# Operands at multiples of 128 bytes, and 64-byte gaps between the homes of the split weights

## The chip, the cores and the metric

The kernel runs on one core of a Trainium2 chip. The metric is the device time of one execution in microseconds. Five engines work side by side: PE (TensorE, matmuls; its weight loads are listed as PEld), DVE (VectorE), ACT (ScalarE), POOL (GpSimd) and SP (SyncE, which issues the DMAs). They meet in SBUF, a memory of 128 partitions in which an operand is a range of bytes in every partition, and in PSUM, where PE puts its sums. This change moves operands within SBUF, so the start of an operand is given here in bytes from the start of the partition.

## The reference

One transformer block on x of 1 x 2048 x 448 in float32: layer norm, attention with 16 query heads of 28 and a single key and value head, residual; layer norm, a gated feed-forward with 1792 hidden columns, residual.

```python
x = A_x
h = x + _A_ref(_layernorm(x), A_wq, A_wk, A_wv, A_wo)
h2 = h + _B_ref(_layernorm(h), B_w1, B_w3, B_w2)
# _A_ref: p = softmax(q k^T * Dh**-0.5); (p v) @ wo
# _B_ref: gate = x @ w1; up = x @ w3; (silu(gate) * up) @ w2
```

## The kernel before

**Tiling.** The 2048 rows are four row tiles of 512 (`T`); the 448 columns are three chunks of 128 and one of 64. To keep nearly float32 accuracy with PE's faster rounded type, most products are made from a split of each operand into a rounded high part and the rest: high x high, low x high and high x low. `mm_D` (line 156) issues these for one output of 128 x 512 as eleven matmuls: three with the high input `xh` and the high weights, three with the low input `xl` and the high weights, three with `xh` and the low weights, and two for the 64-column chunk, in which `xh` holds both parts. PE streams the moving operand (here the input) past the stationary one (here 128 columns of weights); each matmul has its own weight load, which runs while the matmul before it streams.

**Stages.** Projections of q, k and v at the start (line 163 with the output `pb`); attention, where for each of 256 steps the scores of four heads are made from `KS` and the queries `qs` (line 367, each matmul on 32 partitions), ACT takes their exponentials into the tiles `pt`, `xh` and `xl` (line 374) and PE multiplies these with `VA` (line 383); beside that, ahead of time, the row maxima (line 283, then DVE at lines 293 and 311); the output projection (`wo_rows`, also line 163, moving `WO`, stationary `OS`, 448 columns); and from about 752 us on the feed-forward alone.

**The feed-forward.** For each row tile and each of 14 blocks of 128 hidden columns: `split_w` (DVE and POOL) splits the block's 128 columns of w1 and w3 into two homes, one for the high and one for the low part; `ffn1` makes gate (w1) and then up (w3) with 22 matmuls of 512 columns at line 163, moving `xh` and `xl`, the transposed normalised input; ACT and DVE make silu(gate) x up and split it into the tile `pt`; `ffn2` multiplies it with the split w2 (tile `w2s`) in 12 matmuls of 448 columns at line 990, for the block before. All this is written in a fixed order by hand, with splits two blocks ahead.

**Where operands lie.** The pool `keep` lays tiles one behind the other in the order of their first use, each padded to 32 bytes. `qs_tile` (line 84) hands out homes in turn. A home has 4096 bytes per partition; within it the four chunks of a weight block stand 1024 bytes apart, and in each chunk 512 bytes of w1 and then 512 of w3 (`put_w13`, line 88: index `m` 0 and 1). In the feed-forward the order of homes is

```python
homes, n_qs = [5, 6, 1, 2, 3, 4, 0], [0]     # line 945
```

Block 0 takes homes 5 and 6, block 1 homes 1 and 2; then one home goes to a split of w2, and from block 2 on each block takes the next two: 4 and 0, 5 and 6, 1 and 2, 3 and 4, 0 and 5, 6 and 1, 2 and 3, and again from 4 and 0. So home 5 serves blocks 0, 3, 6, 10, 13, 17, 20 and so on, in steps of 3 and 4. The input tiles (`xh`, `xl`, pool `xt`) follow behind the homes; their chunks are 2048 bytes apart.

Before the change `pexp` and `warm_t` hold 16 bytes each. Behind `pexp` everything stands 32 bytes past a multiple of 128; behind `warm_t`, which comes after home 5, it stands 64 past one. In memory the homes lie in the order 5, 6, 0, 1, 4, 2, 3, then the input. Home numbers, and starts by the layout of the built program:

| operand | start before | mod 128 | start after | mod 128 |
|---|---|---|---|---|
| KS, first of two | 45984 | 32 | 46080 | 0 |
| w2s (also KS, second) | 54176 | 32 | 54272 | 0 |
| OS, WO, QR, VA | | 32 | | 0 |
| home 5 | 141984 | 32 | 142080 | 0 |
| home 6 | 146112 | 64 | 146240 | 64 |
| home 0 | 150208 | 64 | 150400 | 0 |
| home 1 | 154304 | 64 | 154560 | 64 |
| home 4 | 158400 | 64 | 158720 | 0 |
| home 2 | 162496 | 64 | 162816 | 0 |
| home 3 | 166592 | 64 | 166976 | 64 |
| xh, first of two | 170688 | 64 | 171136 | 0 |
| pt holding the hidden block | 212416 or 220608 | 64 | 212864 or 221120 | 0 or 64 |

The distance from the input to the weights, modulo 1024, is the same for all chunks, since the chunks of either lie multiples of 1024 apart. Before, it is 0 for w1 and 512 for w3 in six homes, and 992 and 480 in home 5.

Of the kernel before, what the change touches and what calls it, by code (L numbers as in the profile page):

```python
# [8 lines left out]
F32 = mybir.dt.float32  # L9
F32R = mybir.dt.float32r  # L10
AF = mybir.ActivationFunctionType
# [5 lines left out]
P = 128  # L17
# [5 lines left out]
T = 512  # L23
NT = S // T
NQ = T // P
# [10 lines left out]
def block_kernel(  # L36
# [13 lines left out]
    ve, se, ge, pe, sy = nc.vector, nc.scalar, nc.gpsimd, nc.tensor, nc.sync  # L50
# [4 lines left out]
    def f(ap):  # L55
        return ap.bitcast(F32)


    keep = ctx.enter_context(tc.tile_pool(name="keep", bufs=1))
# [7 lines left out]
    X = [keep.tile([P, NQ, D], F32, name=f"X{t}") for t in range(NT)]  # L67
    ident = keep.tile([P, P], F32, name="ident")
    NEG = [keep.tile([P, 32], F32R, name=f"neg{k}") for k in range(2)]
    pexp = keep.tile([P, NQ], F32, name="pexp")  # L70
    KS = [keep.tile([P, S], F32R, name=f"KS{k}", tag=f"ks{k}") for k in range(2)]
    VA = keep.tile([P, NC, 32], F32, name="VA")
    QR = [keep.tile([P, NG, T], F32, name=f"QR{t}") for t in range(NT)]
# [9 lines left out]

    def qs_tile():
        k, n_qs[0] = homes[n_qs[0] % len(homes)], n_qs[0] + 1
        return keep.tile([P, 2, T], F32R, name="qs", tag=f"q{k}")

    def put_w13(k, tl):
        fl = tl.rearrange("p a b -> p (a b)")
# [53 lines left out]
    def bank(name="pb"):  # L143
        k = min(free, key=lambda k: order[k])
        free.remove(k)
        ps = ps_w.tile([P, T], F32, name=name, tag=f"bank{k}")
        used[id(ps)] = ps, k
        ready.pop(id(ps), None)
        return ps

    def done(ps, at=None):
        k = used.pop(id(ps))[1]
        order[k] = ready.get(id(ps), clock.end) + 0.7 if at is None else at
        free.append(k)

    def mm_D(ps0, ps, lhs, rhs, lsl, rsl, between=None, pairs_ab=((0, 0), (1, 0), (0, 1))):

        terms, rsl_n = [], rsl.stop - rsl.start
        for a, b in pairs_ab:
            terms += [(a, c, b, c) for c in range(3)]  # L160
        terms += [(0, 3, 0, 3), (0, 3, 1, 3)]
        for k, (a, ca, b, cb) in enumerate(terms):
            pe.matmul(  # L163
                ps, lhs[b][:, cb, lsl], rhs[a][:, ca, rsl],
                start=(k == 0), stop=(k == len(terms) - 1),
            )
            clock.mm("full", 0, ps0, 0.0182 + rsl_n / 2400, k == 0)
            if between is not None and k == 5:
                between()

    def load_w(dst, w):
        sy.dma_start(dst[:, 0:3], w[0:384].rearrange("(c p) m -> p c m", p=P))
        sy.dma_start(dst[0:64, 3], w[384:448])
        sy.dma_start(dst[64:128, 3], w[384:448])

    def load_w13(k):
        for m, w in enumerate((w1, w3)):
            load_w(W13[k][:, :, m], w[:, k * P : (k + 1) * P])

    def load_w2(k):  # L180
# [32 lines left out]
    XT = {}  # L213
# [43 lines left out]
    def build_qs(i, ps=None):  # L257
        t, g = divmod(i, NG)
        q = QS[i] = qs_tile()
        if ps is None:  # L260
            if i < 3:
                se.activation(q[:, 0], QR[t][:, g], AF.Copy)
            else:
                ge.tensor_copy(q[:, 0], QR[t][:, g])
            ge.tensor_tensor(q[:, 1], QR[t][:, g], f(q[:, 0]), op=ALU.subtract)
        else:
            se.activation(q[:, 0], ps, AF.Copy)
            ve.tensor_tensor(q[:, 1], ps, f(q[:, 0]), op=ALU.subtract)
# [170 lines left out]
    def split_w(k):  # L439
        wh, wl = [qs_tile().rearrange("p a (c m e) -> p (a c) m e", c=2, m=2)  # L440
                  for b in range(2)]
        ve.tensor_copy(wh, W13[k])
        ge.tensor_tensor(wl, W13[k], f(wh), op=ALU.subtract)
        return wh, wl
# [3 lines left out]
    def split_w2(k):  # L448
        if k == 0 and not w2s_home:
            w2s = qs_tile()  # L450
        else:
            if not w2s_home:
                w2s_home.append(keep.tile([P, 2, 2, T], F32R, name="w2s", tag="ks1"))
            w2s = w2s_home[0][:, k % 2]
        ve.tensor_copy(w2s[:, 0, :D], W2[k])
        ge.tensor_tensor(w2s[:, 1, :D], W2[k], f(w2s[:, 0, :D]), op=ALU.subtract)  # L456
        return w2s

    PAIRS = (0, 1)
    KD = keep.tile([P, 2, T], F32R, name="KD", tag="q5")  # L460
    warm_t = keep.tile([P, NQ], F32, name="warm_t")
    KDS = {0: KD[:, 0]}
    ab_t = keep.tile([P, 2, T], F32, name="ab", tag="q6")
    ab_pool, n_ab = [ab_t[:, k] for k in range(2)], [0]
    for h in range(2):
        sy.dma_start(X[0][:, 2 * h : 2 * h + 2], xv[0][:, 2 * h : 2 * h + 2])
    make_identity(nc, ident)
    ge.memset(pexp, -0.5)
    se.activation(warm_t, pexp, AF.Copy)

    with tc.tile_pool(name="start", bufs=1) as sp:
        wq_r = wo_r = OT[:, :, :D]
# [301 lines left out]
    p_pool = ctx.enter_context(tc.tile_pool(name="pt", bufs=1))  # L774
# [1 line left out]
    more, n_pt, n_ring = xt_tiles(), [0, 0], [0]  # L776

    def pt_new(k):
        return p_pool.tile([P, 2, T], F32R, name="pt", tag=f"pt{k}")

    def pt_ring():
        k, n_ring[0] = n_ring[0] % 4, n_ring[0] + 1
        return pt_new(k)

    def pt_tile(p):
        k, n_pt[p] = n_pt[p] % 3, n_pt[p] + 1
        return pt_new(2 * k + p) if k < 2 else more[p][:, :2]
# [36 lines left out]
    for t in range(NT - 1):  # L824
        for k in range(2):
            at(NC * NG * (t + 1) + 13 + k, load_w13, 2 * t + k)
# [144 lines left out]
    def ffn1(t, k, W):  # L971
        ps = [bank("pa"), bank("pa")]
        for m in range(2):
            mm_D(ps[m], ps[m], [w[:, :, m] for w in W], XT[t], slice(0, P), slice(0, T))
        sg = f(pt_ring()[:, 0])
        se.activation(sg, ps[0], AF.Silu)  # L976
        done(ps[0])
        ve.tensor_tensor(sg, ps[1], sg, op=ALU.mult)  # L978
        done(ps[1])
        h = pt_ring()  # L980
        se.activation(h[:, 0], sg, AF.Copy)  # L981
        ve.tensor_tensor(h[:, 1], sg, f(h[:, 0]), op=ALU.subtract)
        HID[t, k] = h[:, 0], h[:, 1]
# [17 lines left out]
    tl = NT - 1  # L1001
# [7 lines left out]
    for k in range(2):  # L1009
        on(0, 2.5, load_w13, 2 * tl + k)  # L1010
# [4 lines left out]
    for k in range(8, NF):  # L1015
        on(0, 2 if k < 10 else 4.5, load_w13, k)
        on(0, 4.5, load_w2, k)
# [8 lines left out]
    for t in range(NT):  # L1026
        for k in range(NF):
            end = t == tl and k >= NF - 2
            t2, k2 = divmod(NF * t + k + 2, NF)
            if t2 < NT:  # L1030
                WH[t2, k2] = split_w(k2)
            ffn1(t, k, WH.pop((t, k)))
            for fn, args in after.get((t, k), []):
                fn(*args)
            if prev is not None and not end:
                for n in range(NQ):
                    ffn2(*prev, n)
                if prev[1] == NF - 1:
                    for n in range(NQ):
                        y_out(prev[0], n)  # L1040
            t2, k2 = divmod(NF * t + k + 1, NF)
            if t2 < NT and not end:
                WS[t2, k2] = split_w2(k2)
            for fn, args in after.get((t, k + 0.5), []):
                fn(*args)
            prev = (t, k)
# [36 lines left out]
```

## Time and profile before

| | us |
|---|---|
| median of 3 runs | 1182.97 |
| lowest and highest | 1182.55 and 1183.31 |
| the profiled execution | 1182.28 |
| its span, first to last instruction | 1180.5 |

| stage, us from the span's start | PE busy | DVE | ACT | POOL |
|---|---|---|---|---|
| 0 to 100, start and first row maxima | 95.30 | 81.75 | 59.91 | 35.50 |
| 100 to 700, attention | 598.70 | 533.51 | 567.84 | 72.29 |
| 700 to 740, its last steps | 39.56 | 3.19 | 39.44 | 9.01 |
| 740 to 752 | 12.00 | 4.49 | 3.69 | 4.69 |
| 752 to 1180, feed-forward | 424.64 | 160.99 | 74.28 | 204.00 |

How to read it: a line of the profile names a source line (L163), an engine, an operation, the tiles written and read (`pa<-xh,qs`: moving xh, stationary qs, into PSUM tile pa) and a count. Matmuls follow one another while the one before still drains, so what a matmul costs is the distance from its start to the next start, not its own length. The chain of waits, listed in order of time, gives these distances summed over a stretch of equal matmuls.

### The profile page before, as it was taken

The page shows a single profiled execution, that of the slowest core. Times are in us where ns is not written, and L with a number is a line of the kernel's source. Part 1 is how long each engine was busy: PE and PEld are TensorE (multiplying, and loading weights), DVE is VectorE, ACT ScalarE, POOL GpSimd, SP SyncE. Part 2 cuts the span into 40 slices and gives each one's busy share as a digit, 9 for nine tenths or more (in the row PEclk, how much of TensorE's full clock was granted, in tenths as well). Part 3 has the DMA queues.
Part 4 walks back from the last instruction along what each step waited for, and adds up shares of the span by engine and source line. Part 5 has one row for each costly group of instructions (what it writes and reads, how often), then busy time and mean ns, then how long its engine had stood idle before and what let it go on. Part 6 is the DMA issues. An engine that isn't in the chain of part 4 may idle for free.

```text
span 1180.5 us, 22184 instructions
## 1 busy us (share of the span) xinstructions
PE 1170.2 (99%) x8618; PEld 746.3 (63%) x8618; DVE 783.9 (66%) x1479; ACT 745.2 (63%) x1435; POOL 325.5 (28%) x240
## 2 busy tenths in 40 slices
PE   8999999999999999999999999999999999999998
PEld 6664444446444445444455443788888888888887
DVE  8878999997999988989987961544343333433332
ACT  5649999996999997999998999312111111211111
POOL 5312001111110111110013013344555545455552
PEclk9999999999999999999999999999999999999999
DMA  4010100011000011000011000242000000000000
GB/s 165 10 37 2 42 12 9 19 24 37 19 19 10 12 23 38 19 19 17 5 42 35 2 18 19 79 114 59 1 32 1 1 24 9 1 1 32 1 1 31
DMA packets 35050, 30.58 MB, mean 26 GB/s; under 512 B 11905, under 2 KB 29569, under 8 KB 34945
## 3 DMA queue, kind: packets, MB, share of 16 engines
q1 hardware_dynamic: 34944, 29.17, 8.6%
q8 instruction: 67, 1.10, 0.4%
q14 instruction: 39, 0.31, 0.1%
HBM read 20.37 MB, written 3.80 MB: 20 GB/s over the span
## 4 chain that ended last, share of the span: by engine, by line
PE 95%; ACT 2%; DVE 2%; issue 1%; DMA 0%; POOLq 0%; POOL 0%; ACTq 0%
PE pa L163 27%; PE po L383 21%; PE pb L367 19%; PE pb L990 11%; PE pa L283 11%; PE pb L163 4%; PE pb L238 1%; ACT OT L390 1%; ACT ab L304 1%; ACT pt L374 0%; DVE mx L293 0%; DMA X<-in_A_x_dram 0%; DVE X L994 0%; ACT xh L374 0%; DVE st L192 0%
## 5 line engine op out<-in xcount | busy, mean ns | idle before, releaser
L293 DVE TENSOR_REDUCE mx<-pa 128x1 f32<-128x512 f32 x689 | 440.3, 685 | 22.6 <-PE pb L367 13.1
L367 PE MATMUL pb<-qs,KS 32*128 32x512 f32 x3072 | 385.4, 425 | 0.0
L374 ACT ACTIVATE pt<-pb 128x512 f32<-128x512 f32 x684 | 366.3, 622 | 12.5 <-PE pb L367 9.2
L367 PEld LDWEIGHTS pb<-qs,KS 32*128 32x128 f32 x3072 | 234.1, 182 | 132.6 <-ACT pt L374 68.1
L283 PE MATMUL pa<-KS,qs 32*128 32x512 f32 x886 | 312.1, 459 | 1.3
L163 PE MATMUL pa<-xh,qs 128*128 128x512 f32 x896 | 232.7, 392 | 0.0
L283 PEld LDWEIGHTS pa<-KS,qs 32*128 32x128 f32 x886 | 139.0, 182 | 83.7 <-DVE mx L293 46.5
L163 PEld LDWEIGHTS pa<-xh,qs 128*128 128x128 f32 x896 | 168.1, 188 | 35.4 <-issue 0.8
L383 PE MATMUL po<-pt,VA 128*32 128x512 f32 x1368 | 182.2, 604 | 0.4 <-ACT pt L374 0.4
L978 DVE TENSOR_TENSOR pt<-pa,pt 128x512 f32<-128x512 f32 x56 | 38.7, 691 | 209.3 <-PE pa L163 204.6
L976 ACT ACTIVATE pt<-pa 128x512 f32<-128x512 f32 x56 | 33.5, 597 | 195.1 <-PE pa L163 195.0
L990 PE MATMUL pb<-w2s,pt 128*128 128x448 f32 x660 | 145.0, 368 | 0.2 <-POOL w2s L456 0.2
L414 POOL TENSOR_TENSOR OT<-OT,rb 128x512 f32<-128x512 f32 x15 | 19.2, 1281 | 456.0 <-DMA rb<-sd 229.0
L981 ACT ACTIVATE pt<-pt 128x512 fp32r<-128x512 f32 x56 | 35.4, 633 | 153.6 <-DVE pt L978 149.3
L990 PEld LDWEIGHTS pb<-w2s,pt 128*128 128x128 f32 x660 | 122.8, 188 | 13.4 <-POOL w2s L456 0.6
L311 DVE CUSTOM_DVE_ANT_0 ab<-pa,ab 128x512 f32<-128x512 f32 x138 | 93.7, 687 | 39.7 <-PE pa L283 31.8
L374 ACT ACTIVATE xh<-pb 128x512 f32<-128x512 f32 x170 | 104.7, 634 | 0.0
L374 ACT ACTIVATE xl<-pb 128x512 f32<-128x512 f32 x170 | 99.8, 611 | 7.6 <-PE pa L283 5.3
L163 PE MATMUL pa<-xl,qs 128*128 128x512 f32 x336 | 95.1, 391 | 0.0
L383 PE MATMUL po<-xl,VA 128*32 128x512 f32 x340 | 89.4, 605 | 0.0
L383 PE MATMUL po<-xh,VA 128*32 128x512 f32 x340 | 89.4, 605 | 0.0
L304 ACT ACTIVATE ab<-pa 128x512 f32<-128x512 f32 x138 | 82.3, 608 | 6.7 <-PE pa L283 5.0
(109 smaller groups left out, 1084.0 us busy)
## 6 DMA issues: line engine op xcount, KB each, us to landing
rb<-sd SPq DMA_DIRECT2D x64, 64.0 KB
QR<-OT SPq DMA_DIRECT2D x60, 56.0 KB
QR<-in_B_w_dram SPq DMA_DIRECT2D x16, 192.0 KB
X<-in_A_x_dram SPq DMA_DIRECT2D x3, 896.0 KB
out_dram<-X SPq DMA_DIRECT2D x3, 896.0 KB
w<-in_B_w_dram SPq DMA_DIRECT2D x8, 192.0 KB
w_wo<-in_B_w_dram SPq DMA_DIRECT2D x6, 224.0 KB
qs<-mr SPq DMA_DIRECT2D x64, 2.0 KB
```

Source lines behind the costliest of these rows:

```text
L163: pe.matmul(ps, lhs[b][:, cb, lsl], rhs[a][:, ca, rsl], start=(k == 0), stop=(k == len(terms) - 1),)
L283: pe.matmul(ps, QS[i][r, 0, n * P : (n + 1) * P], KS[0][r, kt * T : (kt + 1) * T] if keys is None else keys[r], start=True, stop=True)
L293: ve.tensor_reduce(self.to(), ps, axis=AX.X, op=ALU.max)
L304: se.activation(self.ab, ps, AF.Relu)
L311: ve.tensor_tensor_reduce(self.ab, ps, self.ab, 1.0, -3.0e38, ALU.add, ALU.max, self.to())
L367: pe.matmul(self.ps, KS[k % 2][r, c * P : (c + 1) * P], QS[i][r, k // 2], start=(k == 0), stop=(k == 2))
L374: se.activation(f(PT[i, c, p][:, jj]), self.ps, AF.Exp, bias=0.0, scale=SCALE)
L383: pe.matmul(PO[i][32 * j : 32 * j + 32], VA[:, c], f(PT[i, c, j // 2][:, j % 2]), start=(c == 0), stop=(c == NC - 1))
L976: se.activation(sg, ps[0], AF.Silu)
L978: ve.tensor_tensor(sg, ps[1], sg, op=ALU.mult)
L981: se.activation(h[:, 0], sg, AF.Copy)
L990: pe.matmul(Y[t][n][:, :D], hid[a][:, n * P : (n + 1) * P], w2s[:, b, :D], start=(k == 0 and m == 0), stop=(k == NF - 1 and m == 2))
```

## The change

It does four things. `pexp` grows to 128 bytes and takes the place of `warm_t`, so that what follows it starts at a multiple of 128. A new function `shift` allocates a tile of 64 bytes the first time a home is handed out, for all homes but number 4 and for the first of the `pt` tiles used, so that the next tile starts 64 bytes further. `load_w13` writes w3 into the first half of each chunk and w1 into the second, and `ffn1` reads them with `1 - m`, so that gate is still made first. Nothing else is added or removed: the sequence of instructions on PE, DVE and POOL is the same, ACT's first ACTIVATE writes another tile, and SP issues the loads of w3 ahead of those of w1.

After it, the distance from the input to the weights modulo 1024 is, for w1 and w3: home 5 128 and 640, home 6 192 and 704, home 0 256 and 768, home 1 320 and 832, homes 4 and 2 384 and 896, home 3 448 and 960.

```diff
-    pexp = keep.tile([P, NQ], F32, name="pexp")
+    pexp = keep.tile([P, 32], F32, name="pexp")
...
-        return keep.tile([P, 2, T], F32R, name="qs", tag=f"q{k}")
+        tl = keep.tile([P, 2, T], F32R, name="qs", tag=f"q{k}")
+        shift(keep, k)
+        return tl
+
+    shifted = {4, "pt1", "pt2", "pt3"}
+
+    def shift(pool, k):
+        if k not in shifted:
+            shifted.add(k)
+            pool.tile([P, 16], F32, name=f"gap{k}")
...
-        for m, w in enumerate((w1, w3)):
+        for m, w in enumerate((w3, w1)):
             load_w(W13[k][:, :, m], w[:, k * P : (k + 1) * P])
...
     KD = keep.tile([P, 2, T], F32R, name="KD", tag="q5")
-    warm_t = keep.tile([P, NQ], F32, name="warm_t")
+    shift(keep, 5)
     KDS = {0: KD[:, 0]}
     ab_t = keep.tile([P, 2, T], F32, name="ab", tag="q6")
+    shift(keep, 6)
...
-    se.activation(warm_t, pexp, AF.Copy)
+    se.activation(pexp[:, 8:16], pexp[:, 16:24], AF.Copy)
...
-        return p_pool.tile([P, 2, T], F32R, name="pt", tag=f"pt{k}")
+        tl = p_pool.tile([P, 2, T], F32R, name="pt", tag=f"pt{k}")
+        shift(p_pool, f"pt{k}")
+        return tl
...
-            mm_D(ps[m], ps[m], [w[:, :, m] for w in W], XT[t], slice(0, P), slice(0, T))
+            mm_D(ps[m], ps[m], [w[:, :, 1 - m] for w in W], XT[t], slice(0, P), slice(0, T))
```

## The prediction

> **What bounds the kernel now.** First the page: the shares of the engines, the granted clock, and the chain of work that ended last.
>
> ```profile
> span 1180.5 us, 22184 instructions
> PE 1170.2 (99%) x8618; PEld 746.3 (63%) x8618; DVE 783.9 (66%) x1479; ACT 745.2 (63%) x1435; POOL 325.5 (28%) x240
> PEclk9999999999999999999999999999999999999999
> PE 95%; ACT 2%; DVE 2%; issue 1%; DMA 0%; POOLq 0%; POOL 0%; ACTq 0%
> ```
>
> PE carries 95% of the chain at an ungated clock. A busy PE says little by itself (its matmuls overlap in the record), so next the busy time by stage, where PE, weight loads, DVE, ACT and POOL stand in this order, and then who waited for whom in the feed-forward stage:
>
> ```profile
> 100.00:280.00 180.00, 179.61 (x1755) 84.96 (x1751) 163.40 (x306) 177.12 (x351) 20.12 (x20) 1.00 0.07 18
> 752.00:1180.00 428.00, 424.64 (x1953) 361.56 (x1951) 160.99 (x274) 74.28 (x123) 204.00 (x109) 1.00 0.08 24
> ```
>
> ```profile
> DVE pt L978 <- PE pa L163: 204.6, 51, 4.8
> PEld pb L990 <- POOL w2s L456: 0.6, 1, 0.6
> ```
>
> In attention ACT is busy for 177.12 of 180 us, nearly as long as PE: the two hold each other. In the feed-forward stage (752 to 1180 us) the other engines sit below half busy and wait for PE; PE waits for them 0.6 us in all. There a nanosecond on a matmul is a nanosecond of the kernel, and the question is whether the distance in bytes between a matmul's moving operand and the weights that are loaded under it costs anything. The chain in order of time answers it, since each first product of the feed-forward is one piece of 22 matmuls (start, length, what):
>
> ```profile
> 810.04 5.00 PE pa L163 x22
> 817.92 5.00 PE pa L163 x22
> 825.37 5.09 PE pa L163 x22
> 830.46 2.46 PE pb L990 x12
> 832.92 5.04 PE pa L163 x22
> 840.41 5.04 PE pa L163 x22
> 847.90 5.09 PE pa L163 x22
> 855.45 5.04 PE pa L163 x22
> 877.93 5.08 PE pa L163 x22
> 900.88 5.08 PE pa L163 x22
> 932.09 5.08 PE pa L163 x22
> ```
>
> Identical work takes 5.00, 5.04 or 5.09 us. Split weights walk through seven homes, two for each block of 128 hidden columns, so a given home returns after 3 and 4 blocks in turn. The long pieces come at just that beat: 825.37 is block 10, and from there to 847.90, 877.93, 900.88 and 932.09 it is 3, 4, 3 and 4 blocks. These are the blocks that hold home 5, the only one 32 bytes past a multiple of 128; the other six and the normalised input lie 64 past one. Of the 49 pieces of 22 that stand alone in this view 14 last 5.08 or 5.09 (794.14 to 1143.91), and those are all the blocks with home 5 between them; 28 last 5.04 (802.12 to 1151.45) and 7 last 5.00 (754.53 to 1031.35).
>
> The timeline of PE parts block 10 (first five rows) and block 11 (the rest) by moving operand:
>
> ```profile
> 825.21 0.85 PE L163 MATMUL pa<-xh,qs 128*128 128x512 f32 x3
> 825.90 0.87 PE L163 MATMUL pa<-xl,qs 128*128 128x512 f32 x3
> 826.61 2.02 PE L163 MATMUL pa<-xh,qs 128*128 128x512 f32 x8
> 828.46 0.85 PE L163 MATMUL pa<-xl,qs 128*128 128x512 f32 x3
> 830.30 0.37 PE L990 MATMUL pb<-w2s,pt 128*128 128x448 f32 x1
> 832.76 0.86 PE L163 MATMUL pa<-xh,qs 128*128 128x512 f32 x3
> 833.45 0.85 PE L163 MATMUL pa<-xl,qs 128*128 128x512 f32 x3
> 834.14 2.00 PE L163 MATMUL pa<-xh,qs 128*128 128x512 f32 x8
> 835.98 0.84 PE L163 MATMUL pa<-xl,qs 128*128 128x512 f32 x3
> 836.66 1.29 PE L163 MATMUL pa<-xh,qs 128*128 128x512 f32 x5
> 837.79 0.57 PE L990 MATMUL pb<-w2s,pt 128*128 128x448 f32 x2
> ```
>
> From start to start the first six matmuls, which use the w1 half of the home, take 1.38/6 = 230 ns in block 11 and 1.40/6 = 233 in block 10. The last eight, which use the w3 half 512 bytes on, take 1.81/8 = 226 in block 11 and 1.84/8 = 230 in block 10. So in block 11, where all homes lie a multiple of 1024 bytes from the input, the half at distance 0 (mod 1024) is the slow one and the half at 512 the fast one. In the blocks of 5.00 the first half is fast too (5.00/22 = 227), so distance 0 can lock into the fast beat but mostly doesn't.
>
> The Trainium skill says otherwise: "SBUF — State Buffer", section Who interferes with whom, gives TensorE one read port for the moving operand and one for weight loads, and says that PE and ACT never wait on anyone. By that no address matters and the change is worth nothing. The trace disagrees by the 0.09 us between 5.00 and 5.09.
>
> **The change part by part.** The order of instructions on PE, DVE and POOL stays as it was.
>
> *First product (56 blocks of 22).* All relative offsets become multiples of 64, none of them 0 or 512 (mod 1024): w1 at 128 to 448, w3 at 640 to 960. The mean piece is (7 x 5.00 + 28 x 5.04 + 14 x 5.085)/49 = 5.047 us. If every home now allows the fast beat, 56 x (5.047 - 5.00) = 2.6 us go. If every block runs at block 10's 233 ns, 56 x (22 x 0.233 - 5.047) = 4.4 us come. No row shows a relative offset of 64. I take the gain: the w3 half shows that away from distance 0 the fast beat is taken at once, and the one offset that is known to be slow, 32, goes.
>
> *Second product (660 matmuls of 448 columns).* Now w2s lies 32 and the hidden tile 64 past a multiple of 128: 2.46/12 = 205.0 ns each. The output projection has the same shape, with both operands 32 past one:
>
> ```profile
> 619.55 2.24 PE pa L163 x11
> 622.23 2.24 PE pa L163 x11
> ```
>
> That is 203.6 ns. With offsets of 0 and 64 I take 1.4 x 660 = 0.9 us off; bounds 0 and, if half of them (the hidden tiles at 64) keep the old cost, 0.45.
>
> *Projections at the start (224 matmuls at line 163 into pb).* Their weights lie 32, the input 64 past a multiple of 128, and an undisturbed group of eleven takes
>
> ```profile
> 23.42 2.56 PE pb L163 x11
> 33.37 2.56 PE pb L163 x11
> ```
>
> or 233 ns each; at 227 that is 2.50. All together 224 x 6 = 1.3 us, of which I take half, 0.6, since other groups there wait for ACT and DVE as well; bounds 0 and 1.3.
>
> *Scores in attention.* KS lies 32 and the queries 64 past a multiple of 128. Within a run of score matmuls the chain advances like this, and each run ends in the value product:
>
> ```profile
> 304.63 0.23 PE pb L367 x2
> 301.02 1.01 PE po L383 x8
> ```
>
> A step of 0.23 could fall to the 0.227 of the fast beat. With two to three such steps in a run and some 250 runs that is 0.003 x 2.5 x 250 = 1.9 us at most, and ACT at 98% busy may swallow it: I take 0.9, bounds 0 and 1.9. The value product keeps its distances (four tiles of the same pools, again multiples of 1024 apart).
>
> *The rest costs nothing.* The warming ACTIVATE writes into pexp rather than warm_t, in the shadow of the first load of X; w3 is loaded ahead of w1, but PE's only recorded wait in the feed-forward is the 0.6 us above, on a w2 split. Without that cover one block's loads arriving late would stall PE once, by a few us at most. DVE, ACT and POOL have no part in it: POOL is busy 204.00 of 428 us there.
>
> Sum: 2.6 + 0.9 + 0.6 + 0.9 = 5.0 us. The profiled execution took 1182.28 us, 1180.5 of it span, so 1177.3; it lies 0.7 below the median of 1182.97, so in medians **1178.0 us**.
>
> **The rivals.**
>
> *Addresses don't matter (0.13).* Then 5.00, 5.04 and 5.09 come from something else in the pattern of blocks, and the time stays 1183.0. For it: the rule of the Trainium skill above. Against it: the beat of 3 and 4.
>
> *The grain is 128 bytes, not 64 (0.12).* A relative offset of 64 then costs what 32 costs now. Homes 1, 3 and 6 come to lie at 64: of seven blocks in turn four hold one of them, one holds two, two hold none, hence 4 x 5.09 + 5.14 + 2 x 5.04 = 35.58 against 7 x 5.047 = 35.33 us, 2.0 us more over 56 blocks. The second product gains half (0.45), the scores half (0.45), the start 0.6. Net +0.5: 1183.5. For it: the offset 32 is known to cost, 64 not known to be free.
>
> *Slower: the w3 half loses its fast beat (0.15).* Now 28 of 49 blocks are saved by the distance 512. If the spread of distances puts both halves in reach of a collision, all 22 run at 233 ns: +4.4 us, with nothing won elsewhere 1187.4. It decides as soon as the mean matmul passes 5.047/22 = 229.4 ns. For it: the half at distance 0 holds its slow beat through a whole block. Against it: the blocks of 5.00, where distance 0 is harmless.
>
> *More than the best rows (0.04).* "TensorE: Matmul & The Clock Gate", section Wait — 56ns, not 53.3ns?, of the Trainium skill gives N ÷ 2.4 GHz + 2.5 ns, 215.8 for 512 columns. By that page the gain would be an estimated 56 x 22 x 13.6 ns = 17 us. No piece here, however aligned, gets below 5.00/22. As a mechanism of this kernel: if the distances free a further 5 ns of each, 56 x 22 x 5 = 6 us more go: 1172.
>
> **How the numbers follow.** The forecast has 0.56, the rivals 0.13, 0.12, 0.15 and 0.04. The range of 1174.5 to 1186.5 holds the forecast with all its bounds, the two cases without effect and the nearer part of the slower one; the likeliest case alone spans 1176 to 1180. This kernel's measurement can tell 0.2% (2.4 us) from no change. Faster by more than that: 0.56, less a little for a forecast that is half fulfilled, plus 0.04, say 0.60. Slower: 0.15. The remaining 0.25 is within.
>
> **What would show it.** In the chain of the changed kernel the pieces of 22 at line 163 should nearly all last 5.00, with no beat of 3 and 4; the pieces of 12 at line 990 fall from 2.46 to 2.44; groups of eleven at the start from 2.56 to 2.50. If the long pieces follow homes 1, 3 and 6, the grain is 128. If all pieces last 5.1, the slower rival holds. I am wrong in the main if attention (100 to 740 us) moves by more than the feed-forward does, for there ACT and PE are so close that small shifts in their order may count for more than 1.9 us either way.

## The result, and the profile after

| | before | after |
|---|---|---|
| median of 20 runs, us | 1183.05 | 1184.51 |
| lowest and highest | 1181.90 and 1184.88 | 1183.49 and 1186.17 |
| span of the profiled execution | 1180.5 | 1182.4 |

The ratio after/before is 1.0015, with a 95% interval of 1.0009 to 1.0021. The change costs 1.46 us: a small loss, below the 0.2% that the prediction took as the line, and outside the forecast's own span of 1176 to 1180.

The page of the changed kernel first: span, busy times, and the shares of the chain.

```profile
span 1182.4 us, 22184 instructions
PE 1172.3 (99%) x8618; PEld 747.8 (63%) x8618; DVE 784.0 (66%) x1479; ACT 745.2 (63%) x1435; POOL 326.1 (28%) x240
PE 93%; DVE 3%; ACT 2%; DMA 1%; issue 1%; SPq 0%; POOLq 0%; POOL 0%; ACTq 0%; DVEq 0%
```

The same instructions run, DVE, ACT and POOL are as busy as before, and PE is busy 2.1 us longer (1172.3 against 1170.2). The span is 1.9 us longer, so the loss is PE's own. The busy times by stage say where (attention, then feed-forward; stretch, sum, then PE, weight loads, DVE, ACT, POOL, mean, clock):

```profile
100.00:700.00 600.00, 598.65 (x5679) 295.35 (x5679) 533.34 (x1002) 567.85 (x1120) 72.30 (x72) 1.00 0.08 21
752.00:1180.00 428.00, 426.09 (x1952) 361.97 (x1950) 161.06 (x274) 74.36 (x123) 204.60 (x109) 1.00 0.07 23
```

In attention PE stays at 598.65 (598.70 before). In the feed-forward it goes from 424.64 to 426.09 in the same window, with one matmul fewer in it. The clock is full in both. The value products say again, without a window's edges, that attention didn't move. This is their line before (durations in ns: minimum, median, maximum; then the first and the last start in us):

```profile
L383 PE MATMUL po<-pt,VA x1368: 592/593/617, 89.7 to 741.2; 128*32 128x512 f32 x196
```

and after:

```profile
L392 PE MATMUL po<-pt,VA x1368: 592/593/617, 89.4 to 740.9; 128*32 128x512 f32 x196
```

Both begin and end 0.3 us earlier, and between the two starts lie 651.5 us each time. So look at the chain of the changed kernel in the feed-forward, at the blocks that the prediction showed of before (start, length, what):

```profile
825.98 5.10 PE pa L172 x22
831.08 2.41 PE pb L1002 x12
833.49 5.11 PE pa L172 x22
838.60 2.45 PE pb L1002 x12
841.05 5.11 PE pa L172 x22
846.17 2.41 PE pb L1002 x12
848.58 5.12 PE pa L172 x22
```

No piece of 22 lasts 5.00 any more. All 48 that stand alone in this view last 5.08 to 5.12 us (794.57 to 1153.24). The beat of 3 and 4 blocks is gone because every block is now at least as slow as the block with home 5 was. The pieces of 12 fell from 2.46 to 2.41 and 2.45 in turn.

The timeline of PE parts the block at 825.98 as the prediction did with block 11:

```profile
825.82 0.86 PE L172 MATMUL pa<-xh,qs 128*128 128x512 f32 x3
826.51 0.86 PE L172 MATMUL pa<-xl,qs 128*128 128x512 f32 x3
827.21 2.02 PE L172 MATMUL pa<-xh,qs 128*128 128x512 f32 x8
829.07 0.86 PE L172 MATMUL pa<-xl,qs 128*128 128x512 f32 x3
829.77 1.31 PE L172 MATMUL pa<-xh,qs 128*128 128x512 f32 x5
830.92 0.36 PE L1002 MATMUL pb<-w2s,pt 128*128 128x448 f32 x1
```

From start to start the first six take 1.39/6 = 232 ns and the last eight 1.85/8 = 231. Before, in block 11, the last eight took 226. Both halves have lost the fast beat, the steps of 226 to 227 ns.

Summing the distances from start to start of all matmuls, by what precedes what, gives the whole 1.9 us. Steps over 245 ns stand apart, as waits:

| us | before | after | difference |
|---|---|---|---|
| first product within blocks, 1177 steps | 270.00 | 273.12 | +3.12 |
| second product, 602 steps | 123.02 | 121.68 | -1.34 |
| last of second to first of first product | 10.48 | 10.29 | -0.19 |
| last of first to first of second product | 9.09 | 9.24 | +0.15 |
| steps over 245 ns in the second product | 5.03 | 5.47 | +0.44 |
| attention, first value product to feed-forward | 652.07 | 652.05 | -0.02 |
| start, up to the first value product | 89.66 | 89.40 | -0.26 |

The +0.44 is one wait, for the hidden tile of block 1:

```profile
760.13 2.48 PE L1002 MATMUL pb<-w2s,pt 128*128 128x448 f32 x11 [0.49 <-DVE pt L994]
```

It is one event in one profiled execution. The row varies without any gaps too: it is 5.77 in e7 below. What is to be explained is the first row: a matmul of the first product went from 270.00/1177 = 229.4 to 232.0 ns, although the one offset that was known to be slow is gone.

### The profile page after: what moved, and what is told of

The parts are those of the page before. It is cut to its first block, busy times and chain, and to the rows that moved or that the text cites. A ratio compares the mean times of both kernels' runs of the same rounds, so it can differ in the third digit from the quotient of the medians.

```text
span 1182.4 us, 22184 instructions
## 1 busy us (share of the span) xinstructions
PE 1172.3 (99%) x8618; PEld 747.8 (63%) x8618; DVE 784.0 (66%) x1479; ACT 745.2 (63%) x1435; POOL 326.1 (28%) x240
## 4 chain that ended last, share of the span: by engine, by line
PE 93%; DVE 3%; ACT 2%; DMA 1%; issue 1%; SPq 0%; POOLq 0%; POOL 0%; ACTq 0%; DVEq 0%
PE pa L172 26%; PE po L392 21%; PE pb L376 20%; PE pb L1002 11%; PE pa L292 10%; PE pb L172 4%; PE pb L247 1%; DVE mx L302 1%; ACT OT L399 1%; ACT ab L313 1%; ACT pt L383 0%; DMA sd<-sm 0%; DMA X<-in_A_x_dram 0%; DVE pt L994 0%; DVE X L1006 0%
## 5 line engine op out<-in xcount | busy, mean ns | idle before, releaser
L172 PE MATMUL pa<-xh,qs 128*128 128x512 f32 x896 | 235.1, 395 | 0.0
```

The lines of the kernel that those rows point to most:

```text
L172: pe.matmul(ps, lhs[b][:, cb, lsl], rhs[a][:, ca, rsl], start=(k == 0), stop=(k == len(terms) - 1),)
```

## The experiments

"Distance" means the bytes from the moving operand to the weights modulo 1024, for the two halves: in the first product from input to w1 and w3, in the second from w2s to the hidden tile. Two starts are called out of step by 32 if they differ by 32 modulo 64. Means are per matmul, from start to start, without steps over 245 ns. Where the last column says "one run", the time is that of a single execution; the others have a median. Single executions of the kernel before lie up to 3.0 us apart (1181.90 to 1184.88), so a single time settles large differences alone. The means are steadier: the 1177 steps of the first product sum to 267.97, 267.99 and 268.00 us in e1, e2 and e7.

| kernel | first: distance | ns | second: distance | ns | us | ratio to before |
|---|---|---|---|---|---|---|
| before | 0/512; home 5 992/480 | 229.4 | 544/32 | 204.4 | 1183.05 | |
| after | 128/640 to 448/960 | 232.0 | 896/384 and 960/448 | 202.1 | 1184.51 | 1.0015 |
| e1 | 0/512 | 227.7 | 512/0 | 203.1 | 1179.84 | 0.9976 (0.9966 to 0.9985) |
| e2 | 512/0 | 227.7 | 512/0 | 203.2 | 1179.97 | 0.9975 (0.9965 to 0.9985) |
| e3 | as after, halves in old order | 232.0 | as after | 202.1 | 1184.37 | one run |
| e4 | 768/256 | 227.7 | 768/256 | 203.1 | 1178.93 | one run |
| e5 | 960/448 | 229.6 | 576/64 | 202.1 | 1181.33 | one run |
| e6 | 896/384 | 232.9 | 640/128 | 204.0 | 1186.69 | one run |
| e7 | 0/512, all 32 past 128 | 227.7 | 512/0 | 203.1 | 1179.88 | 0.9975 (0.9966 to 0.9985) |
| e8 | 0/512 | 227.2 | 960/448 | 200.0 | 1176.49 | 0.9946 (0.9934 to 0.9959) |
| e9 | 0/512; home 5 768/256 | 227.7 | 768/256 | 203.1 | 1180.11 | one run |
| e10 | 768/256 | 227.2 | 960/448 | 200.0 | 1176.75 | 0.9949 (0.9936 to 0.9963) |
| e11 | 0/512 | 226.8 | 544/32 | 203.6 | 1178.88 | one run |
| e12 | as before | 229.4 | 0/512 | 202.5 | 1182.00 | one run |
| e13 | 0/512, w2s out of step by 32 | 228.7 | 768/256 | 205.4 | 1183.99 | one run |
| e14 | 0/512, all 64 past 128 | 227.2 | 512/0 | 202.5 | 1179.18 | one run |

**Which part of the change costs: e1, e2, e3.** e1 makes the alignment alone: pexp of 128 bytes, no warm_t, no gaps, the halves in their old order.

```diff
-    pexp = keep.tile([P, NQ], F32, name="pexp")
+    pexp = keep.tile([P, 32], F32, name="pexp")
-    warm_t = keep.tile([P, NQ], F32, name="warm_t")
-    se.activation(warm_t, pexp, AF.Copy)
+    se.activation(pexp[:, 8:16], pexp[:, 16:24], AF.Copy)
```

> Alignment alone: pexp at 128 bytes, warm_t gone, no gaps, halves in the old order; all operands start at multiples of 128, w1 at distance 0 and w3 at 512 (mod 1024) in all seven homes. Theory (the distance modulo 1024 sets the beat, 512 gives the fast one at once, 0 now and then): pieces of 22 at 5.04 or 5.00, none at 5.09, mean matmul of the first product 228.7 ns against 229.4 before; the second product at 202.6 ns a matmul as in the output projection, against 204.4; about 2.3 us below before, 1180.8. Rival (alignment to 128 is itself harmful): pieces at 5.10 as in the changed kernel, 1184.5. Rival (addresses do not matter): 1183.0.

e2 is e1 with the halves exchanged, so that the first half of each block lies at 512 and the second at 0.

```diff
-        for m, w in enumerate((w1, w3)):
+        for m, w in enumerate((w3, w1)):
-            mm_D(ps[m], ps[m], [w[:, :, m] for w in W], XT[t], slice(0, P), slice(0, T))
+            mm_D(ps[m], ps[m], [w[:, :, 1 - m] for w in W], XT[t], slice(0, P), slice(0, T))
```

> Alignment and the exchanged halves, no gaps: w1, which is used first, at distance 512 and w3 at 0. Theory, with the addition that distance 0 holds a beat in which it is entered: the first half falls into the fast beat at once and the second keeps it, pieces of 22 at 5.00, mean 227.0 ns, about 4 us below before, 1179.0. Rival (each half has its own rate, whatever went before): the halves trade places and pieces stay at 5.04, 1180.8. Rival (the exchange of the halves is what cost the changed kernel its time): pieces above 5.04 and a time not below that of alignment alone.

e3 is the changed kernel with just this exchange undone.

```diff
-        for m, w in enumerate((w3, w1)):
+        for m, w in enumerate((w1, w3)):
-            mm_D(ps[m], ps[m], [w[:, :, 1 - m] for w in W], XT[t], slice(0, P), slice(0, T))
+            mm_D(ps[m], ps[m], [w[:, :, m] for w in W], XT[t], slice(0, P), slice(0, T))
```

> The changed kernel with the halves in the old order, so w1 at 640 to 960 and w3 at 128 to 448. Theory (no half at distance 512): pieces of 22 stay at 5.08 to 5.12, mean 232.0 ns. Rival (the exchange is the cause): pieces back at 5.04, mean 229.

The alignment alone is a gain: 1179.84 against 1182.78 of the kernel before beside it. Its chain:

```profile
841.23 5.00 PE pa L163 x22
846.24 2.43 PE pb L989 x12
848.67 5.00 PE pa L163 x22
```

36 of its pieces of 22 last 5.00. The timeline of its block at 826.21 shows both halves fast:

```profile
826.21 0.86 PE L163 MATMUL pa<-xh,qs 128*128 128x512 f32 x3
826.90 0.84 PE L163 MATMUL pa<-xl,qs 128*128 128x512 f32 x3
827.58 1.98 PE L163 MATMUL pa<-xh,qs 128*128 128x512 f32 x8
829.39 0.84 PE L163 MATMUL pa<-xl,qs 128*128 128x512 f32 x3
830.07 1.30 PE L163 MATMUL pa<-xh,qs 128*128 128x512 f32 x5
```

The first six take 1.37/6 = 228 ns at distance 0. With the halves exchanged the mean stays 227.7, not the 227.0 that was expected: in e2 the first three steps of a block take 232 ns each as in e1, though they now lie at 512. Undoing the exchange in the changed kernel leaves 232.0. So distance 0 and 512 are equally good, the exchange does nothing, and what costs in the changed kernel is the gaps, by which alone it differs from e2: 273.12 - 1177 x 0.2277 = 5.1 us in the first product.

**Which distances are fast: e4, e5, e6.** Each is e1 with one gap ahead of the normalised input, so that all homes keep one common distance to it. Only this gap differs: 256 bytes in e4 (shown), 64 in e5 (`[P, 16]`) and 128 in e6 (`[P, 32]`).

```diff
     homes, n_qs = [5, 6, 1, 2, 3, 4, 0], [0]
+    keep.tile([P, 64], F32, name="gap")
```

> Alignment, no gaps between homes, one gap of 256 bytes ahead of the input: w1 at 768 and w3 at 256 in all homes, every offset a multiple of 256. Theory (only 512 takes the fast beat by itself): both halves at 231 to 232 ns, pieces about 5.10. Rival (offsets of an odd multiple of 64 are what costs): pieces at 5.00 to 5.04.

> Alignment, no gaps between homes, one gap of 64 bytes ahead of the input: w1 at 960 and w3 at 448 in all homes, one distance throughout, 192 past a multiple of 256. Theory G (the grain: the fast beat of 226.7 ns exists only at distances that are multiples of 256): no block settles, mean of the first product 231 to 233 ns, pieces about 5.10. Theory N (the spread: any one distance that is a multiple of 64 settles, and the changed kernel never does because it changes distance with every home): pieces at 5.00 to 5.04, mean 227.7. The second product, at 576 and 64: near 202 by either.

> The same with a gap of 128 bytes: w1 at 896 and w3 at 384 in all homes, all starts multiples of 128. Theory G: no block settles, mean 231 to 233 ns, pieces about 5.10. Theory N, or a grain of 128: mean 227.7, pieces at 5.00 to 5.04. The second product, at 640 and 128, by the rows of the changed kernel at 896 and 384: 204.

The chain of e4, with a gap of 256 bytes:

```profile
824.58 5.00 PE pa L163 x22
829.58 2.43 PE pb L990 x12
832.01 5.00 PE pa L163 x22
```

of e5, with 64:

```profile
848.09 5.05 PE pa L163 x22
853.14 2.43 PE pb L990 x12
855.56 5.05 PE pa L163 x22
```

and of e6, with 128:

```profile
849.51 5.12 PE pa L163 x22
854.63 2.44 PE pb L990 x12
857.08 5.12 PE pa L163 x22
```

A shift of 256 costs nothing (5.00), so it is not a matter of 0 and 512 alone; 64 costs 0.05 on each block, half of what was expected, and 128 costs 0.12. The 7.8 us between e4 (1178.93) and e6 (1186.69) come from 128 bytes ahead of the input; 6.2 of them lie in the first product, whose steps sum to 267.99 and 274.18 us. This also takes away the thought that the spread is at fault: in e6 every home has the same distance, and it is slower than the changed kernel. What counts is the distance modulo 256, and 0 is the only fast one that was found for the first product (64, 128, 192 and, with home 5, 224 are slow).

With that the changed kernel can be read matmul by matmul, its own weights and the next ones taken together. Where both lie at 0 modulo 256 from the input (home 0, 112 steps), a step takes 229.5 ns; at 192 (homes 6 and 3, 214 steps) 230.1; at 128 (homes 5, 4 and 2, 339 steps) 232.7; at 64 (home 1, 118 steps) 233.4; the 394 steps from one distance to another 229.6 to 234.8. That is the order of e4, e5 and e6, and even home 0, one of seven, doesn't reach 227.7 between its neighbours.

**Does the start itself matter: e7, e14.** e7 (shown) gives pexp 32 bytes and e14 64 bytes (`[P, 16]`), with no warm_t and the warming ACTIVATE within pexp: all operands lie 32 (e7) or 64 (e14) past a multiple of 128, with the distances of e1.

```diff
-    pexp = keep.tile([P, NQ], F32, name="pexp")
+    pexp = keep.tile([P, 8], F32, name="pexp")
-    warm_t = keep.tile([P, NQ], F32, name="warm_t")
```

> No operand at a multiple of 128: warm_t is gone and pexp holds 32 bytes, so that everything behind it, the homes, the input and w2s included, stands 32 bytes past one, with the relative distances of alignment alone (0 and 512 in the first product, 512 and 0 in the second). Theory (only the distance between the two operands counts): as alignment alone, mean 227.7 and 203.1 ns, about 1180. Rival (the start itself must be a multiple of 64 or 128): the first product at 229 to 234 ns, 1182 or more.

> Alignment's distances, with every start behind pexp 64 past a multiple of 128. Theory (only distances count): as alignment alone and as the kernel with all starts 32 past, pieces of 22 mostly 5.00, mean 227.7 ns. Rival (a start 64 past a multiple of 128 is what made the run-ins of the kernel before long): mostly 5.04, mean 228.7.

1179.88 (0.9975) and 1179.18 against e1's 1179.84: the gain doesn't need starts at multiples of 128. In e14 both means are even lower (227.2 and 202.5 ns against 227.7 and 203.1), in one run; why was not tried. The gain of e1 comes from taking away warm_t, which had put home 5, w2s and the attention operands out of step by 32 with all that lies behind: e7, in which pexp takes up the 32 bytes that it took up before, does just this.

**The second product and a version that is faster: e8, e9, e10.** In the changed kernel the pieces of 12 alternate with the two hidden tiles: 2.41 where the distance is 960/448, 2.45 where it is 896/384. e8 gives both tiles the better one, by 448 bytes ahead of the first tile of the `pt` pool, on top of e1.

```diff
+    p_pool.tile([P, 112], F32, name="gap")
```

> Alignment alone, with one gap of 448 bytes ahead of the pt tiles: the first product stays at distances 0 and 512, the second goes from 512 and 0 to 960 and 448. By the changed kernel's rows, where hidden tiles at 960 and 448 took 200.4 ns and those at 896 and 384 took 204: the second product falls from 203.1 to 200.4 ns, 660 x 2.7 = 1.8 us below alignment alone, about 1178. Rival (those 200.4 ns came from the homes or from the tiles' change from block to block, not from the distance): 203 ns and 1180.

e9 puts 256 bytes between home 5 and the other homes, on top of e1: the spread of distances that the change makes, but in steps of 256.

```diff
-    warm_t = keep.tile([P, NQ], F32, name="warm_t")
+    keep.tile([P, 64], F32, name="gap")
```

> Alignment, with a single gap of 256 bytes behind home 5: its w1 lies at 768 and its w3 at 256, the other six homes stay at 0 and 512, so the distance changes whenever home 5 comes round. Theory (the grain is 256, and a change of distance within it is free): the blocks with home 5 last 5.00 or 5.04 like the others, mean 227.7 ns. Rival (a change of distance from home to home throws the beat): the blocks with home 5, in steps of 3 and 4, stand out by 0.02 us or more.

e10 joins the input's shift of e4 with the second-product distance of e8.

```diff
+    p_pool.tile([P, 48], F32, name="gap2")
...
+    keep.tile([P, 64], F32, name="gap")
```

> Alignment, a gap of 256 bytes ahead of the input and one of 192 ahead of the pt tiles: the first product at 768 and 256, the second at 960 and 448, the projections at the start at 512 and 0. Theory: the feed-forward as with the gap of 448 alone (429.4 us from its first to its last matmul, first product 227.2 ns, second 200.0), the start like that with the gap of 256 (89.1 us to the first value product), so 1176.4. Rival (the 448 kernel's fast first product needs distances 0 and 512): first product back at 227.7 ns, 1177 or more.

The chain of e8:

```profile
846.45 4.99 PE pa L163 x22
851.43 2.40 PE pb L990 x12
853.83 4.99 PE pa L163 x22
858.82 2.40 PE pb L990 x12
```

1176.49 against 1182.88 of before beside it, 0.9946: 6.4 us, and the best of all versions; it beats both kernels. 37 of its pieces of 22 last 4.99 and 39 of those of 12 last 2.40. It is 3.4 us faster than e1, where 1.8 was expected. The second product gives 1.8 (its 602 steps sum to 122.26 us in e1 and 120.42 in e8), and the first another 0.5, since in 37 blocks its slow first steps are gone: the distance within the second product reaches into the first. e10 agrees (1176.75): with the input shifted by 256 both means stay. e9 has the mean of e1 (227.7) and no beat of home 5: different distances do no harm if they are multiples of 256.

**What made the first half slow before: e11, e12, e13.** The kernel before had distance 0 in most blocks and still took 5.04, not 5.00. In e1 too the first matmuls of a block are slower than the later ones, in most blocks for three steps (232 ns each), and in the kernel before for some ten. The second product was one suspect: e11 puts its distance in e1 back to that of before (32 bytes ahead of `pt`, shown); e12 gives the kernel before the distance 0/512 there (480 bytes, `[P, 120]`).

```diff
+    p_pool.tile([P, 8], F32, name="gap")
```

> Alignment, with a gap of 32 bytes ahead of the pt tiles, so that the second product lies at 544 and 32 as before the change, while the first keeps 0 and 512 and starts at multiples of 128. Theory (the 5.04 of the kernel before is a run-in of up to ten matmuls after the second product, whose length hangs on the beat the second product ends in, not on the distance of the first half): pieces of 22 mostly back at 5.04, pieces of 12 at 2.46. Rival (the 5.04 came from the first product's own places, 64 past a multiple of 128): pieces of 22 stay mostly at 5.00, pieces of 12 at 2.46.

> The kernel before with nothing but a gap of 480 bytes ahead of the pt tiles: the first product stays at 0 and 512 in six homes, 64 past a multiple of 128, and at 992 and 480 in home 5; the second goes from 544 and 32 to 0 and 512. Theory (run-in): blocks without home 5 mostly at 5.00 instead of 5.04, those with home 5 still longer, about 5.05, pieces of 12 at 2.43. Rival (the first product's places): blocks without home 5 stay mostly at 5.04.

The theory missed in both. The chain of e11 keeps 5.00 and 4.99, and its first product has the lowest mean of all (226.8):

```profile
825.14 5.00 PE pa L163 x22
830.13 2.43 PE pb L990 x12
839.99 4.99 PE pa L163 x22
```

and that of e12 stays at 5.03 and, with home 5 in the block, 5.11:

```profile
818.50 5.03 PE pa L163 x22
825.97 5.11 PE pa L163 x22
831.07 2.43 PE pb L991 x12
833.50 5.03 PE pa L163 x22
```

So the distance within the second product doesn't make the 5.04. What both leave is that before, w2s (32 past 128) and the homes and input (64 past) are out of step by 32 where PE goes over from the second product to the first. e13 makes just this, beginning from e7: 96 bytes ahead of home 5 put homes and input at 0, while KS and w2s stay at 32; 160 bytes ahead of `pt` make the second product's distance 768/256.

```diff
+    keep.tile([P, 24], F32, name="gap")
     KD = keep.tile([P, 2, T], F32R, name="KD", tag="q5")
...
+    p_pool.tile([P, 40], F32, name="gap2")
```

> Inside each product all distances are multiples of 256 (first product 0 and 512, second 768 and 256), but w2s and pt start 32 past a multiple of 128 and the homes and the input at 0, so that the weight loads at the change from the second to the first product are out by 32. Theory (the run-in is long when the two products are out of step with each other): pieces of 22 mostly 5.03 to 5.04, pieces of 12 at 2.43. Rival (places inside each product decide): pieces mostly 5.00.

The chain of e13:

```profile
826.94 5.04 PE pa L163 x22
831.99 2.47 PE pb L991 x12
834.46 5.04 PE pa L163 x22
```

5.04 is back in a kernel that has the good distance 0/512 in all homes, and the timeline has the slow first half again:

```profile
826.78 0.87 PE L163 MATMUL pa<-xh,qs 128*128 128x512 f32 x3
827.49 0.85 PE L163 MATMUL pa<-xl,qs 128*128 128x512 f32 x3
828.18 1.99 PE L163 MATMUL pa<-xh,qs 128*128 128x512 f32 x8
830.00 0.84 PE L163 MATMUL pa<-xl,qs 128*128 128x512 f32 x3
```

The first six take 1.40/6 = 233 ns. The second product is slow as well (2.47), at a distance that costs 2.43 in e4. Its time, 1183.99 beside 1183.25 for before, holds 1.0 us of a later first value product (90.62 against 89.66), a sum that scatters from 89.07 to 90.62 over all these kernels; so the pieces are compared and not the times. So w2s out of step by 32 with the homes and the input, at the change of product, is enough to make nine or ten matmuls slow: e13 has this in all 49 blocks of 22 that begin behind a full piece of the second product. This is not the only thing that brings it. In e1, where nothing is out by 32, 11 of these 49 blocks show it too, and each stands behind a second product that four transposes (L238) precede:

```profile
808.04 0.44 PE pb L238 x4
808.48 2.47 PE pb L989 x12
810.95 5.04 PE pa L163 x22
```

e2, e4, e7, e8, e9 and e10 have 11 blocks behind transposes like this, too. In the kernel before it is the other way round: six of the seven pieces of 5.00, those at 810.04 and 817.92 among them, stand behind these transposes. So the number of slow steps also hangs on how PE came into the second product. Why is open.

## Why the prediction was wrong

Point by point, by its own steps:

- *PE alone bounds the feed-forward, and a nanosecond on a matmul is one of the kernel:* right. The 1.9 us of the span are found in PE's steps, and DVE, ACT and POOL moved by at most 0.6 us of busy time.
- *The block with home 5 is slow because it lies 32 out of step:* right. e1 takes this away and the 5.09 goes; e12 keeps it and has 5.11.
- *"All relative offsets become multiples of 64 ... I take the gain":* this step failed. It was priced at -2.6 us and measured +3.1. A multiple of 64 isn't enough; the first product is fast at multiples of 256 only (e4 against e5 and e6), and the gaps move six of seven homes off one. The step rested on "the half at distance 0 (mod 1024) is the slow one and the half at 512 the fast one". The two halves of a block differ in distance, but also in order: the half at 0 runs first, right behind the second product. e2 exchanges the distances and the mean stays, so it was the order, and e13 shows what the order brings in: the change of operands out of step by 32. The blocks of 5.00 spoke against the reading, and the prediction said so without drawing the conclusion; six of the seven follow the transposes, so what went before decided there too, and not the distance. It had bounded the unknown from -2.6 to +4.4, and the answer lay near the end that it didn't take.
- *Second product, -0.9:* right in sign, -1.34 measured, but in the main not for its reason. The assumption that one distance of multiples of 64 is like another fell again: the hidden tile at 960/448 takes 2.41, the one at 896/384 takes 2.45 and so hardly less than the 2.46 of 544/32. What the 32 itself costs is between 0.5 ns a matmul (203.6 in e11 against 203.1 in e1) and 1.9 (204.4 before against 202.5 in e12).
- *Start, -0.6:* not found. The -0.26 lies within the scatter from 89.07 to 90.62 just told of, and an undisturbed group of eleven stays at 2.56 in the changed kernel. In e1 the same group (at 23.41) takes 2.51, near the 2.50 that was hoped for. By the layout of the built programs its weights lie a multiple of 256 from the input in e1, and 128 off one in the changed kernel, so the step that failed in the first product failed here too.
- *Scores, -0.9:* nothing. Attention takes 652.05 us after 652.07, with a full clock. Whether ACT hides it or the score matmuls don't care was not tried. Nor do the value products keep their distances, as the prediction had it: by the layout their `pt` tiles lay 32 past `VA` modulo 128 and now lie 0 or 64 past it. It made no difference: 1793 steps from one value product to the next sum to 121.55 us before and 121.57 after.
- *Warming ACTIVATE and order of loads at no cost:* for the order of loads right by e3 (1184.37 with the old order). The ACTIVATE was not changed alone; the first value product comes no later with it (89.40 after 89.66).
- *The rivals:* the slower one named the right stage and the right sign in the chain (all pieces near 5.1), at +4.4 where +3.1 was measured. Its mechanism, a collision that the spread of distances brings, falls with e9, where a spread costs nothing, and e6, where no spread costs most. The rival with a grain of 128 had the right kind of cause with too fine a grain; that its 1183.5 lies nearest to the measured 1184.51 is luck, since it takes 128 for harmless, and e6 shows that 128 is dear (5.12). That a matmul could get faster than the best rows (1172) falls too: no first product settled below 226.7 ns in any run. That addresses don't matter falls with e4 and e6. The Trainium skill's rule in "SBUF — State Buffer", section Who interferes with whom, by which PE's two reads don't disturb each other, would make those two kernels alike; they differ by 7.8 us, so here the measurement decides against it.

Taken apart, the change is an alignment that gains 1182.78 - 1179.84 = 2.9 us (e1) and gaps that lose 5.1 us in the first product and gain 602 x (203.1 - 202.1 ns) = 0.6 us in the second: 2.9 - 5.1 + 0.6 is a loss of 1.6 us, and 1.46 was measured.

## What to carry to other kernels

When matmuls run back to back and PE alone sets the end, lay the moving operand and the weights loaded beneath it a multiple of 256 bytes apart (shown here for 512 columns on 128 x 128 weights), and keep the operands of the neighbouring products in step with them; where in memory all of them start mattered by 0.7 us at most (e14, one run). Try the distance of each product by itself, with one gap ahead of one pool, since the 448-column product had another best distance (960/448) than the 512-column one. Before two rows are read as two addresses, ask what else differs between them: here it was the order.

## What the runs showed of the hardware

- The fast beat, once settled, was 226.7 ns for 512 columns and 200.0 for 448. The 64 columns between them take 26.7 ns, 0.417 each, which leaves an estimated 226.7 - 512 x 0.417 = 13 ns of each matmul that don't depend on its length. No operand layout that was tried got below that.
- Off the fast distance a settled run doesn't take one longer step but a pattern: 226, 229, 232 ns at 64 bytes off (e5), 229 and 238 in turn at 128 (40 of 49 blocks of e6).
- After the change from the second to the first product it takes three steps in most blocks of e1 to fall into the fast beat, none in 37 blocks of e8 and of e11, and nine or ten if w2s and the first product's operands are out of step by 32 (e13 and, in most blocks, before) or, in e1, if four transposes preceded the second product.
- At the same distance modulo 256 the sign counts: in the changed kernel 192 takes 230.1 ns and 64 takes 233.4 (home 1 alone; no run gave all homes 64).

What in the memory makes a distance fast, and why the second product prefers 448 and 960 to multiples of 256 (200.0 against 203.1), stays open.
